# Moving small exponentials and a tiny transpose out of the start-up of a fused layer-norm, state-space and gated-linear kernel

## Chip, cores, metric

One core of one Trainium2 chip. The metric is the device time of one execution in microseconds (us), the median of several runs. Each ratio is taken against the kernel before in the same call.

Names: PE is the matmul engine, PEld its weight loads, DVE the vector engine, ACT the scalar (activation) engine, POOL GpSimd, SP the engine that only issues DMAs here.

## The reference, cut to what matters

```python
xn = layernorm(x)                       # x: 2048 x 576
# A: diagonal state-space layer
dt      = exp(log_dt)                   # 576 values
Lam_bar = exp(dt * (Lambda_re + 1j*Lambda_im))
B_bar   = ((Lam_bar - 1) / Lam)[:, None] * Bmat
h[t]    = Lam_bar * h[t-1] + B_bar @ xn[t]
A       = 2 * Re(Cmat @ h) + xn * Dskip
# B: gated linear unit
B       = (sigmoid(xn @ w_gate) * (xn @ w_up)) @ w_down      # 576 -> 4608 -> 576
out     = x + A + B
```

The modulus of `Lam_bar` is `exp(dt * Lambda_re)`: 576 numbers, held as a tile `r5` of 128 x 5 (`r` in the views). It is first read when the tables of sines are combined, long after the start.

## The kernel before

The gate/up matmuls of the first groups start as soon as the first two of 16 row tiles of x are normalised and transposed. PSUM holds four pairs of banks; each group of 128 hidden columns takes a pair, and ACT frees it by writing sigmoid(gate) and then u = xn @ w_up to SBUF. In the views, `pgu` is the PSUM of a group, `ptr` that of the transposes and `pd` that of the down product; `sT` and `uT` are ACT's two outputs, and `crows` and `cvals` the constants before and after their transposes. The program order of the start (cuts marked `...`):

```python
def consts_transpose(ps):          # log_dt, Lambda_re, Lambda_im: 27 rows of 64 -> columns
    for half in (slice(0, H), slice(H, P)):
        nc.tensor.transpose(ps[half, 0:3 * NH], crows[:], ident[0:3 * NH, 0:3 * NH])

def exp_first():
    nc.scalar.activation(dt[:], ldt, ACT.Exp)
    for a in range(NU):                                            # NU = 5
        nc.scalar.activation(r5[:, a:a + 1], lre[:, a:a + 1], ACT.Exp, scale=dt[:, a:a + 1])
...
busy(10, TB)                       # filler matmuls, so that PE reaches full speed
busy(6, P)
for tt in range(2):
    ln_stats(tt); ln_std(0, tt, tt + 1)
for tt in range(2):
    ln_recip(0, tt, tt + 1); ln_norm(tt, twice=False); start_transpose(tt)
busy(20, P)
start_copy(0, ...); ...            # ACT and DVE copy the transposes to xT
start_groups[0].mms(slice(0, 2 * P))
start_transpose(2); start_transpose(3)
start_groups[1].mms(slice(0, 2 * P))
...
start_groups[0].mms(slice(2 * P, TB))
consts_transpose(ptrs[1][:, NH, :])
consts_copy(ptrs[1][:, NH, :])     # DVE
start_groups[1].mms(slice(2 * P, TB))
for tt in range(TT_B, 2 * TT_B):
    ln_stats(tt)                   # DVE: statistics of the second block of x
for g in start_groups:
    g.evac()                       # ACT: sigmoid, copy of u; DVE: product
ln_std(1, 0, TT_B)                 # ACT: square root
exp_first()                        # ACT
...                                # then the other groups, f = 2, 3, ...
```

Far later, in the first down phase (`pd` matmuls, where ACT has little to do), `sines()` computes eleven sines on ACT.

## Time and profile before

| | before |
|---|---|
| median of the first three runs | 508.32 us (508.27 to 509.04) |
| span in the profile | 506.7 us |
| PE busy | 501.5 us |
| steady places where PE waits | one, at 22 us |

The prediction shows the lines that carry this. One more view will serve as a ruler: the timeline restricted to PE, from 9.3 us to the first down phase (its first row, the rest of group 0's first matmuls, is left out). Columns: start us, duration us, engine, line, operation, number merged, idle before and its cause.

```profile
9.79 1.20 PE L747 MATMUL ptr<-ident,xn 128*64 128x128 bf16 x36
10.92 2.14 PE L501 MATMUL pgu<-xT,wgu 64*128 64x256 bf16 x36
12.99 0.20 PE L196 MATMUL ptr<-ident,crows 27*64 27x27 bf16 x2
13.12 8.93 PE L501 MATMUL pgu<-xT,wgu 64*128 64x256 bf16 x90
22.88 35.14 PE L501 MATMUL pgu<-xT,wgu 64*128 64x512 bf16 x324 [0.83 <-ACT uT L508]
57.95 1.28 PE L575 MATMUL pd<-wd,hT 128*128 128x288 bf16 x9
```

From 10.92 on PE has work in hand without a break, except for the small transposes (L196) and the stop. I call the stretch from the first of these rows with L501 (10.92) to the first `pd` matmul (57.95) the stream. Its length is 57.95 - 10.92 = 47.03 us. It leaves out the start-up before it.

### The profile page before, as it was taken

To read this page: it belongs to the slowest core of one execution; us is meant where nothing else is said; L and a number is where in the kernel's file an instruction comes from. 1 tells how busy PE (TensorE), PEld (TensorE's weight loads), DVE (VectorE), ACT (ScalarE), POOL (GpSimd) and SP (SyncE) were. 2 spreads that over 40 slices of the span, in tenths; PEclk is the share of its full clock that TensorE was granted. 3 is DMA by queue.
4 is the path that set the end of the run, shared out by engine and by line. 5 is a ranking of instruction groups with operands and counts; after the bars stand their busy time and mean duration, and the time that the engine had idled before them with its cause. 6 is when DMAs were issued, how large, how long until landed. Compare 5 with 4: busy or idle time off the path is not lost.

```text
span 506.7 us, 10667 instructions
## 1 busy us (share of the span) xinstructions
PE 501.5 (99%) x4538; PEld 292.5 (58%) x4538; DVE 324.7 (64%) x705; ACT 204.4 (40%) x371; POOL 90.8 (18%) x134
## 2 busy tenths in 40 slices
PE   8999999999999999999999999999999999999997
PEld 6455675444477444467764444774444774446775
DVE  5799788887888587868588667786675222222111
ACT  4965723556500756530016655005655005553000
POOL 7116320123110043110001331100431001300000
PEclk9999999999999999999999999999999999999999
DMA  8897594065220096342340652100643200600101
GB/s 224 195 163 218 147 210 94 6 159 136 50 51 25 1 171 150 78 107 69 71 107 2 164 141 49 47 25 1 160 107 86 49 25 24 187 1 1 36 25 35
DMA packets 40949, 45.59 MB, mean 90 GB/s; under 512 B 28614, under 2 KB 32326, under 8 KB 40902
## 3 DMA queue, kind: packets, MB, share of 16 engines
q0 software_dynamic: 10608, 34.22, 27.5%
q1 hardware_dynamic: 29862, 10.37, 10.2%
q8 instruction: 35, 0.57, 0.5%
q10 hardware_dynamic: 432, 0.33, 0.2%
q14 instruction: 12, 0.10, 0.1%
HBM read 34.36 MB, written 2.36 MB: 72 GB/s over the span
## 4 chain that ended last, share of the span: by engine, by line
PE 97%; ACT 1%; DVE 1%; issue 0%
PE pgu L501 54%; PE pd L575 34%; PE pbu L530 7%; PE pd L583 1%; PE pgu L739 1%; DVE bnst L230 1%; PE ptr L747 0%; ACT xT L750 0%; ACT L507 0%; ACT L334 0%; ACT r L336 0%; DVE mv L231 0%; ACT uT L508 0%; ACT rstd L234 0%; DVE ob L584 0%
## 5 line engine op out<-in xcount | busy, mean ns | idle before, releaser
L501 PE MATMUL pgu<-xT,wgu 64*128 64x512 bf16 (+1 forms) x2628 | 284.1, 373 | 0.9 <-ACT uT L508 0.8
L501 PEld LDWEIGHTS <-wgu 64*128 64x128 bf16 x2628 | 130.2, 94 | 149.4 <-issue 1.6
L575 PE MATMUL pd<-wd,hT 128*128 128x288 bf16 x1128 | 141.3, 286 | 0.0
L507 ACT ACTIVATE sT<-pgu 128x512 bf16<-128x512 f32 x144 | 86.5, 600 | 120.0 <-PE pgu L501 119.1
L575 PEld LDWEIGHTS <-hT 128*128 128x128 bf16 x1128 | 109.9, 98 | 30.1 <-issue 0.8
L510 DVE TENSOR_TENSOR hT<-sT,uT 128x512 bf16<-128x512 bf16 x144 | 60.7, 422 | 95.0 <-ACT uT L508 94.7
L508 ACT CAST uT<-pgu 128x512 bf16<-128x512 f32 x144 | 84.2, 585 | 0.0
L154 POOL DMA_DIRECT2D wgu<-in_B_w_gate_dram x36 | 27.6, 766 | 236.4 <-PE pgu L501 224.7
L536 ACT COPY bure<-pbu 128x512 f32<-128x512 f32 x16 | 9.4, 585 | 88.8 <-PE pbu L530 75.0
L160 POOL DMA_DIRECT2D wd<-in_B_w_down_dram x36 | 26.3, 733 | 98.9 <-PE pd L575 98.8
L595 DVE TENSOR_TENSOR acc<-acc,pd 128x576 f32<-128x576 f32 x32 | 24.1, 752 | 27.6 <-PE pd L575 27.6
L592 DVE TENSOR_TENSOR ob<-acc,pd 128x576 bf16<-128x576 f32 x15 | 11.3, 755 | 40.9 <-PE pd L575 40.9
L530 PE MATMUL pbu<-xT,bt 64*128 64x512 bf16 x288 | 33.7, 376 | 0.0
L575 PEld LDWEIGHTS <-hst 128*128 128x128 bf16 x270 | 26.4, 98 | 6.7
L154 POOL DMA_DIRECT2D wgu<-in_B_w_up_dram x36 | 26.5, 736 | 1.3 <-DMA wgu<-in_B_w_up_dram 1.3
L445 DVE TENSOR_TENSOR_SCAN gre<-r,g0re,wrim 128x512 bf16<-128x512 f32 x20 | 25.6, 1279 | 0.1
L575 PE MATMUL pd<-ctre,hst 128*128 128x288 bf16 x120 | 24.5, 286 | 0.0
L575 PE MATMUL pd<-ctim,hst 128*128 128x288 bf16 x120 | 24.5, 286 | 0.0
L530 PEld LDWEIGHTS <-bt 64*128 64x128 bf16 x288 | 13.8, 94 | 17.1 <-issue 0.7
L452 DVE TENSOR_TENSOR_SCAN gim<-r,g0im,wrim 128x512 bf16<-128x512 f32 x16 | 20.4, 1276 | 0.0
L230 DVE BATCH_NORM_STATS2 bnst<-xt 128x6 f32<-128x288 bf16 x32 | 12.5, 432 | 2.3 <-DMA xt<-in_A_x_dram 2.3
L432 DVE TENSOR_TENSOR tq<-T,buim 128x512 bf16<-128x512 bf16 x20 | 13.7, 685 | 0.0
(117 smaller groups left out, 279.9 us busy)
## 6 DMA issues: line engine op xcount, KB each, us to landing
wgu<-in_B_w_gate_dram POOLq DMA_DIRECT2D x36, 288.0 KB, 4.1
wgu<-in_B_w_up_dram POOLq DMA_DIRECT2D x36, 288.0 KB, 4.7
wd<-in_B_w_down_dram POOLq DMA_DIRECT2D x36, 288.0 KB, 5.5
out_dram<-ob SPq DMA_DIRECT2D x15, 144.0 KB, 1.8
xt<-in_A_x_dram SPq DMA_DIRECT2D x10, 144.0 KB, 2.7
xt<-in_A_x_dram POOLq DMA_DIRECT2D x4, 144.0 KB, 6.7
bt<-ctre POOLq DMA_DIRECT2D x2, 288.0 KB, 6.0
bt<-ctim POOLq DMA_DIRECT2D x2, 288.0 KB, 7.5
```

The source lines that it names most:

```text
L154: eng.dma_start(w[rows, :, :], src[:, fs].rearrange("(c p) f -> p c f", p=H))
L160: nc.gpsimd.dma_start(wd[:], B_w_down[f0:f0 + FP * P, :].rearrange("(n p) d -> p n d", p=P))
L230: nc.vector.bn_stats(st[:, gi, :], xt[:, gi * DH:(gi + 1) * DH])
L445: nc.vector.tensor_tensor_scan(gre[:], r_bc, w[:, 0, :], g0re[:, col], ALU.mult, ALU.add)
L452: nc.vector.tensor_tensor_scan(gim[:], r_bc, w[:, 1, :], g0im[:, col], ALU.mult, ALU.add)
L501: nc.tensor.matmul(self.ps[:, gi, cols], w[rows, c, fs], xT[self.nb][rows, c, cols], start=c == 0, stop=c == NH - 1)
L507: nc.scalar.activation(sT[:], self.ps[:, 0, :], ACT.Sigmoid)
L508: nc.scalar.copy(uT[:], self.ps[:, 1, :])
L510: nc.vector.tensor_mul(h[:], sT[:], uT[:])
L530: nc.tensor.matmul(out, w, xT[self.nb][rows, c, ts_], start=c == 0, stop=c == NH - 1)
L575: nc.tensor.matmul(out, lhsT, rhs[:, a * DH:(a + 1) * DH], start=i == 0, stop=i == n - 1)
L595: nc.vector.tensor_add(halves(acc[:]), halves(acc[:]), pd[:, :, 0:DH])
```

## The change

Intent: take work that nobody needs yet off ACT's and DVE's way to the release of a PSUM pair. `exp(log_dt)` stays in front (DVE's angles need dt); `exp(dt*re)` becomes one DVE product in background work and one exponential ahead of the sines; the transposes of the constants run among the filler matmuls, so that DVE need not wait for them at 13 us.

```diff
     def exp_first():
         nc.scalar.activation(dt[:], ldt, ACT.Exp)
-        for a in range(NU):
-            nc.scalar.activation(r5[:, a:a + 1], lre[:, a:a + 1], ACT.Exp, scale=dt[:, a:a + 1])
 
     def angles_small():
+        nc.vector.tensor_mul(r5[:], dt[:], lre)
@@
     def sines():
+        nc.scalar.activation(r5[:], r5[:], ACT.Exp)
@@
-    busy(20, P)
+    consts_transpose(ptrs[1][:, NH, :])
+    busy(18, P)
@@
     start_groups[0].mms(slice(2 * P, TB))
-    consts_transpose(ptrs[1][:, NH, :])
     consts_copy(ptrs[1][:, NH, :])
```

## The prediction

> **What bounds the kernel now.** I read the busy shares first, then PE's waits, the chain that ended last, and the timeline around the one place where PE waits. From the page:
>
> ```profile
> PE 501.5 (99%) x4538; PEld 292.5 (58%) x4538; DVE 324.7 (64%) x705; ACT 204.4 (40%) x371; POOL 90.8 (18%) x134
> ```
>
> PE is busy for 501.5 of 506.7 us. A change that adds or removes no matmul of the main loop can win only where PE stands still. The list of waits names one such place in steady work:
>
> ```profile
> PE pgu L501 <- ACT uT L508: 0.8, 1, 0.8
> ```
>
> The same list restricted to PE after 25 us is empty: from there to the tail nothing that another engine does delays a matmul. So only the first 25 us count. The chain, in order of time, shows how they end (start, us, what):
>
> ```profile
> 10.99 2.07 PE pgu L501 x36
> 13.06 0.15 PE ptr L196 x2
> 13.21 0.02 issue
> 13.23 0.17 DVE cvals L201
> ...
> 17.32 0.22 DVE mv L231
> 17.54 0.02 issue
> 17.57 0.30 ACT rstd L234
> 17.87 0.02 issue
> 17.88 1.28 ACT L334
> ...
> 19.42 0.04 ACT r L336
> ...
> 20.46 1.28 ACT L507
> ...
> 22.25 0.59 ACT uT L508
> 22.84 0.04 issue
> 22.88 35.14 PE pgu L501 x324
> ```
>
> Read it backwards. PE resumes at 22.88 when ACT has copied out u of group f=2, because group f=6 needs that PSUM pair (four pairs: the two transpose tiles take the first two, groups 0 and 1 the others, f=2 to f=5 follow round, f=6 reuses the pair of f=2). ACT was late because it ran, in order, the square root of the second block's deviations, a table load, six exponentials and a table load. The square root was late because DVE had stood still for the constants' transpose, which PE ran only after the second half of group 0. Both parts of the change lie on this one chain.
>
> The timeline, cut to ACT and DVE rows (start, us, engine, line, idle before), gives the durations:
>
> ```profile
> 13.23 0.17 DVE L201 CAST cvals<-ptr 64x15 f32<-64x15 bf16 x1 [0.96 <-PE ptr L196]
> 17.57 0.30 ACT L234 ACTIVATE rstd<-mv,eps_t 128x4 f32<-128x4 f32 x1 [0.87 <-DVE mv L231]
> 19.18 0.21 ACT L334 ACTIVATE dt<-cvals 128x5 f32<-128x5 f32 x1
> 19.42 1.03 ACT L336 ACTIVATE r<-cvals,dt 128x1 f32<-128x1 f32 x5
> ```
>
> **What PE really loses.** The 0.83 us of idle in the record counts from the modelled end of the last matmul. By starts it is more: asked in narrow windows, matmuls of 512 columns start in pairs 0.216 us apart, the last pair before the stop at 21.66, so the next was due at 21.88. It started at 22.88: 1.00 us lost. In the same way the constants' transposes: the last pair of group 0 starts at 12.79, pairs of 256 columns come every 0.11, so the next was due at 12.90; it started at 13.12. The two tiny transposes cost PE 0.22 us there.
>
> **What the Trainium skill says.** "ScalarE: Activation LUTs", section What ACT_TABLE_LOAD costs: a load takes about 1283 ns and a drain of about 1380 ns comes with it. The trace agrees on the load (1.28 us each) but not on a drain: the load for L334 begins at 17.88, 0.01 after the square root ends, and dt starts at 19.18, 0.02 after the load. I use 1.28. The same section has back-to-back ACTIVATEs with one pointer operand at 280 ns, less 93 ns of overlap; the five here take 1.03/5 = 0.206 us each, near that difference. The section "Table sets: the hidden batching unit" says to batch by set, not to return to one: the change goes against this (Exp is used in two places now), so I charge one more load. "TensorE: Matmul & The Clock Gate", section Back-to-back issue gap, has 518 cycles for 512 columns, 0.216 us at 2.4 GHz; the pairs' starts agree.
>
> **The change part by part.**
>
> Part A, exponentials. Removed from the early ACT sequence: five at 1.03 us in all. Kept: dt (0.21) and both table loads, Exp and back to Sigmoid (1.28 each), so most of that block stays. On the way to the release of f=2's pair: -1.03 us. Added: one DVE product of 128x5 in the background work of the first group phase. Its neighbour, dt times lim, takes 0.16 us at 38.14, where PE waits for nothing: 0 on the path. Added in the first down phase: a load of Exp's set (1.28) and one exponential of 128x5 (0.21), so the ten sines of 128x512 come about 1.5 us later. There ACT has 16.89 us of idle after the sines (row of the next load, at 83.78). DVE first wants r5 and the small sines at 64.72; these were done at 60.75 and will be at about 62.3. Its first table product at 66.90 needs the first two large sines, then done by about 63.4; the last of ten moves from 66.88 to 68.4, and its reader comes after 79. All slack is over 2 us: 0 on the path.
>
> Part B, constants' transposes. They go from after group 0's second half to the filler ahead of group 0, in exchange for two filler matmuls of about 0.06 us. PE is 0.22 us shorter at 13 us. In the filler they may add 0.22 - 0.12 = 0.1, but the last filler starts at 8.40 and group 0 only at 8.70, after ACT's copy of xT ends at 8.66; 0.1 fits in. Their data were issued on the SP queue by 2.74; loads of that queue take 2.9 us to land, so about 5.6, before 7.3.
> DVE's 0.96 us of idle goes: the copies can start at 12.29 behind the last xT copy. The statistics follow without gaps, so their end moves from 17.54 to about 16.6. The x tiles issued by POOL from 4.53 to 6.2 land in at most 6.8 us, by 13.0 at the latest; the first is read at about 12.75 (landed about 11.2), the last at 15.6. No new wait. On ACT the second sigmoid, which waits for group 1, moves forward 0.1 (ACT is busy to 14.20), so the load of Sqrt's set ends at about 16.6 in place of 16.69, and the square root starts at about 16.62 in place of 17.57: -0.95 us.
>
> **Sum.** Release of the pair: 22.88 - 0.95 - 1.03 = 20.90. PE's need: 21.88 - 0.22 = 21.66. The release comes 0.76 us early, so the stop disappears: PE gains 1.00 + 0.22 = 1.22 us. The 1.98 us saved on ACT are not what is won; PE's own work is the new bound. The following groups need their pairs at intervals of 1.94 us while ACT releases one each 1.0 us, so no later stop forms. Everything after is PE back to back and shifts as a block. 508.32 - 1.22 = 507.10.
>
> Alone, A would give a release at 21.85 against a need at 21.88: gain 1.00. B alone 21.93 against 21.66: stop of 0.27, gain 1.22 - 0.27 = 0.95. So the parts overlap: 1.22, not 1.95.
>
> **Rivals.**
>
> 1. Another wait takes the early place, as the statistics waiting for x tiles in a DMA stage that is over 80% busy from 13 to 23 us. For it: DVE comes 0.94 us earlier. Against: the landing times above, and 0.76 us of margin. If DVE gained nothing, release would be at 21.85 against 21.66: 0.2 of stop, time about 507.3.
>
> 2. The delayed sines stop DVE in the down phase; accumulations come late and PE lacks PSUM. For it: the work of 1.5 us is real, and DVE is busy for 19.4 of 23.7 us there. Against: over 2 us of slack at the first reader and four pairs in rotation. If all of it reached PE: -1.22 + 1.5, 508.6.
>
> 3. The transposes in the filler hold up the first group, by their data or by the switch of tile shape, and push the whole chain. Against: 0.25 us of slack there. If 0.2 leaked, 507.3. A lower clock through two fewer fillers would cost more, but the slices grant full clock throughout and 18 fillers stay.
>
> 4. PE is not really bound after 25 us in a way the chain hides. Against: the empty list.
>
> **Range and chances.** The three runs of before spread from 508.27 to 509.04, two of them 0.05 apart, so a median should repeat within some 0.2; the possible leaks of 0.2 each lie on the slow side, a run in the upper mode adds up to 0.7 to one run only. I take 507.1 us, 506.7 to 507.9. Two per cent are 10.2 us, eight times what is at stake: same 0.98, 0.01 on either side.
>
> **What would show it.** Right: no wait of PE for uT around 22 us; DVE's copies of the constants at about 12.3 without idle; the square root at about 16.6; one ACTIVATE of r 128x5 in the first down phase behind a table load of its own, with ACT idle of about 15.4 us left after the sines; start of the first down phase's matmuls at about 56.7 in place of 57.95; twelve table loads in place of eleven in all. Wrong: a new PE wait below 25 us or between 57 and 84 us; a first matmul of group 0 later than 8.75; a gain of 1.0 or less though the stop is gone, which would mean that the 0.22 of the transposes was paid elsewhere; a gain near 2, which would mean that the release and not PE set the time.

## The result, and the profile after

The changed kernel took 507.58 us (median of 6 runs, 507.21 to 507.84) against 508.65 us (6 runs, 508.27 to 509.04) for the kernel before. The ratio is 0.9979, interval 0.9966 to 0.9992: 1.07 us. Ratios here and below are the mean time of one kernel's runs over that of the other's of the same rounds, so not quite the ratio of the quoted medians.

The page of the changed kernel, first row, to be held against PE's 501.5 us:

```profile
PE 500.9 (99%) x4536; PEld 289.6 (57%) x4536; DVE 324.6 (64%) x706; ACT 204.8 (40%) x368; POOL 90.8 (18%) x134
```

PE's timeline of the changed kernel from 9.3 us, the same view as above:

```profile
10.12 1.20 PE L747 MATMUL ptr<-ident,xn 128*64 128x128 bf16 x36
11.25 45.86 PE L501 MATMUL pgu<-xT,wgu 64*128 64x256 bf16 x450
57.04 2.13 PE L575 MATMUL pd<-wd,hT 128*128 128x288 bf16 x16
```

The transposes at 13 us and the stop are gone; 450 matmuls run as one piece. The stream is 57.04 - 11.25 = 45.79 us, 1.24 us shorter. But it starts 0.33 us later. The reason stands in the timeline from 6 to 24 us (PE, ACT and DVE rows, cut):

```profile
5.96 1.23 PE L747 MATMUL ptr<-ident,xn 128*64 128x128 bf16 x36
...
7.79 0.20 PE L196 MATMUL ptr<-ident,crows 27*64 27x27 bf16 x2 [0.60 <-DMA crows<-in_A_Lambda_im_dram]
...
8.03 0.69 ACT L750 COPY xT<-ptr 128x640 bf16<-128x640 bf16 x1 [0.22 <-PE ptr L196]
...
9.04 1.16 PE L501 MATMUL pgu<-xT,wgu 64*128 64x256 bf16 x18
...
12.52 0.16 DVE L201 CAST cvals<-ptr 64x15 f32<-64x15 bf16 x1
...
16.85 0.30 ACT L234 ACTIVATE rstd<-mv,eps_t 128x4 f32<-128x4 f32 x1
17.17 1.28 ACT L334 ACT_TABLE_LOAD   x1
...
18.46 0.21 ACT L334 ACTIVATE dt<-cvals 128x5 f32<-128x5 f32 x1
18.67 1.28 ACT L507 ACT_TABLE_LOAD   x1
...
20.46 0.58 ACT L508 CAST uT<-pgu 128x512 bf16<-128x512 f32 x1
```

In this execution the constants' loads landed late, PE waited 0.60 us for them in the filler, and group 0 started at 9.04. Behind that, all goes as foreseen: DVE copies the constants without idle, the square root starts without waiting for the statistics, and u of group f=2 is out at 21.04.

What the change added in the first down phase, ACT's timeline from 57 to 84 us, without its first two rows:

```profile
58.24 1.28 ACT L359 ACT_TABLE_LOAD   x1
59.54 0.21 ACT L359 ACTIVATE r<-r 128x5 f32<-128x5 f32 x1
59.75 1.28 ACT L360 ACT_TABLE_LOAD   x1
61.05 0.31 ACT L360 ACTIVATE sc<-sc,zero_t 128x20 f32<-128x20 f32 x1
61.26 6.22 ACT L364 ACTIVATE sctab<-sctab,zero_t 128x512 f32<-128x512 f32 x10
82.87 1.28 ACT L507 ACT_TABLE_LOAD   x1 [15.38 <-PE pgu L501]
```

One load and one exponential more, 15.38 us of idle left. The list of PE's waits names nothing after 8 us.

So two questions went to the chip. Is the sum of the prediction right (two overlapping gains, then PE's own work as the bound)? And does the new place of the transposes cost time regularly, or was the wait of 0.60 us a matter of this one execution?

### The profile page after: what moved, and what is told of

It is laid out like the page before. It is cut to its first block, busy times and chain, and to the rows that moved or that the text cites. A ratio compares the mean times of both kernels' runs of the same rounds, so it can differ in the third digit from the quotient of the medians.

```text
span 505.7 us, 10662 instructions
## 1 busy us (share of the span) xinstructions
PE 500.9 (99%) x4536; PEld 289.6 (57%) x4536; DVE 324.6 (64%) x706; ACT 204.8 (40%) x368; POOL 90.8 (18%) x134
## 4 chain that ended last, share of the span: by engine, by line
PE 98%; DMA 1%; SPq 0%; issue 0%; DVE 0%
PE pgu L501 55%; PE pd L575 34%; PE pbu L530 7%; DMA crows<-in_A_Lambda_im_dram 1%; PE pd L583 1%; PE ptr L747 0%; PE pgu L739 0%; SPq L139 0%; SPq L192 0%; DVE ob L584 0%; PE ptr L196 0%
## 5 line engine op out<-in xcount | busy, mean ns | idle before, releaser
L501 PEld LDWEIGHTS <-wgu 64*128 64x128 bf16 x2628 | 127.7, 94 | 150.9 <-issue 0.5
L431 DVE TENSOR_TENSOR wrim<-T,bure 128x512 bf16<-128x512 bf16 x20 | 13.7, 684 | 0.0
```

What stands on the lines that cost most here:

```text
L431: nc.vector.tensor_mul(w, t1, a[:])
L501: nc.tensor.matmul(self.ps[:, gi, cols], w[rows, c, fs], xT[self.nb][rows, c, cols], start=c == 0, stop=c == NH - 1)
```

## Experiments

Before the single runs, the ruler over all profiles. The release of the pair that group f=6 takes is the moment when ACT has emptied it; the need is the moment when PE would start on it if nothing held it. The need is the start of the stream plus 10.73 us (in run e8 below the stream starts at 11.07 and the pair after the last unhindered one was due at 21.80).

| run | stream starts | stream length | against 47.03 | median time | ratio to before |
|---|---|---|---|---|---|
| before | 10.92 | 47.03 | | 508.65 | |
| e12, before again | 11.09 | 47.03 | 0 | 508.70 (one run) | |
| the change | 11.25 | 45.79 | -1.24 | 507.58 | 0.9979 |
| e5, the change again | 11.32 | 45.79 | -1.24 | 507.40 | 0.9975 |
| e1, exponentials alone | 11.31 | 46.02 | -1.01 | 507.88 | 0.9984 |
| e2, transposes alone | 11.52 | 45.95 | -1.08 | 507.97 | 0.9986 |
| e3, constants' loads earlier | 13.97 | 46.30 | -0.73 | 508.61 | 1.0015 |
| e4, transposes in PE's gap | 10.86 | 45.79 | -1.24 | 507.33 | 0.9977 |
| e6, 6 fillers | 10.76 | 45.79 | -1.24 | 507.28 | 0.9974 |
| e7, 4 exponentials back | 10.74 | 46.54 | -0.49 | 507.41 | 0.9977 |
| e8, 9 exponentials | 11.07 | 46.69 | -0.34 | 508.21 | 0.9992 |
| e9, short first fillers | 12.51 | 45.79 | -1.24 | 508.16 | 0.9986 |
| e10, e4 and e9 together | 12.39 | 45.79 | -1.24 | 508.17 | 0.9992 |
| e11, later sines | 10.85 | 45.79 | -1.24 | 507.35 | 0.9977 |

Where nothing holds it, the stream repeats to 0.01 us. Its start moves by up to 0.8 us between profiles with the same opening (10.74 in e7, 11.52 in e2): that is where the scatter of the times sits. All experiments gave correct results.

### e1, the exponentials alone

```diff
+    busy(20, P)
-    consts_transpose(ptrs[1][:, NH, :])
-    busy(18, P)
@@
+    consts_transpose(ptrs[1][:, NH, :])
     consts_copy(ptrs[1][:, NH, :])
```

(against the changed kernel)

> Only the exponentials are moved; the constants' transposes stay at 13 us. Theory L (the filler position makes PE wait about 0.6 us for the constants' loads, which eats what part B gives): the stop before f=6 goes (release about 21.85 against a need of 21.88), gain 1.0 us over before, so as fast as the whole change within 0.15 us; group 0 starts 2.5 us after the first transpose as before, no PE wait for crows. Rival S (the sum of the prediction holds, 1.22, and 0.3 of it was lost to scatter of the start): gain 1.0 as well, but then the whole change measured in the same call should be 0.2 us faster than this.

PE's timeline of e1:

```profile
11.31 2.14 PE L501 MATMUL pgu<-xT,wgu 64*128 64x256 bf16 x36
13.38 0.20 PE L196 MATMUL ptr<-ident,crows 27*64 27x27 bf16 x2
13.51 43.89 PE L501 MATMUL pgu<-xT,wgu 64*128 64x256 bf16 x414
57.33 1.89 PE L575 MATMUL pd<-wd,hT 128*128 128x288 bf16 x14
```

The stop is gone and the transposes at 13 us remain. The stream is 46.02 us: 1.01 won of the 1.00 predicted for this part. It is 0.23 us longer than the changed kernel's, which is the cost of the two transposes in that place (0.22 predicted). Here the start was late without any wait for the constants: the first transposes began at 6.27 and took 1.37 us. By the clock e1 won 0.8 us (ratio 0.9984, interval 0.9972 to 0.9996), less than the ruler says; by the sum above, that is a start 0.2 us later on average (an estimate from the mean times).

### e2, the transposes alone

```diff
     def exp_first():
         nc.scalar.activation(dt[:], ldt, ACT.Exp)
+        for a in range(NU):
+            nc.scalar.activation(r5[:, a:a + 1], lre[:, a:a + 1], ACT.Exp, scale=dt[:, a:a + 1])
 ...   # and the DVE product and the late exponential taken out again
```

> Only the constants' transposes are moved; six exponentials stay in front. Theory L: PE waits about 0.6 us for crows in the filler as in the changed kernel, the square root starts without waiting for the statistics, release about 1.03 us later than in the changed kernel, a stop of about 0.1 us at f=6; gain over before 0.6 to 0.9 us. Rival S: gain 0.95 us with a stop of 0.27 us and no or a shorter wait for crows. If the parts simply added, this would gain 0.1 to 0.2 us only.

The list of PE's waits showed none at 22 us, but the starts of pairs did; PE's timeline of e2, asked in two narrow windows that overlap the same matmuls (the first row merges the pair at 22.03 with one of the next pair):

```profile
22.03 0.74 PE L501 MATMUL pgu<-xT,wgu 64*128 64x512 bf16 x3
22.40 0.39 PE L501 MATMUL pgu<-xT,wgu 64*128 64x512 bf16 x2
```

Pairs come every 0.216 us, so the one after 22.03 was due at 22.25; it came at 22.40. A stop of 0.15 us is there, hidden in the record by the modelled end of the matmul before it. The stream is 45.95 us: 1.08 won, against 0.95 predicted with a stop of 0.27. Alone the parts win 1.01 and 1.08, together 1.24: they overlap as predicted, and adding them (2.09) would be wrong.

### e3, the constants' loads issued earlier

```diff
-    for tt in range(TT_B):
-        load_x(tt, nc.sync if tt % 2 == 0 else nc.scalar)
+    for tt in range(2):
+        load_x(tt, nc.sync if tt % 2 == 0 else nc.scalar)
+    crows = ...  # its three loads on the SP queue, moved up from below
+    for tt in range(2, TT_B):
+        load_x(tt, nc.sync if tt % 2 == 0 else nc.scalar)
```

> The whole change, with the three small loads of the constants issued between the two x tiles of the SP queue in place of after them, so about 0.5 us earlier and ahead of more of the weights. Theory L: the wait of PE for crows shrinks from 0.60 us to 0.2 or nothing, group 0 starts 2.5 to 2.7 us after the first transpose (3.08 in the changed kernel, 2.50 before), gain over before 1.2 to 1.5 us. Rival S: the start stays as it is, 1.07 us over before. Risk: x tile 2 lands about 0.9 us later, but it is read only at 6.4 us.

508.61 us (6 runs, 508.38 to 510.99), ratio 1.0015: a miss. There are two kinds of runs: four of 508.38 to 508.65 and two of 510.82 and 510.99. The profile is of the 510.82. Its timeline (SP, PE and DVE rows, cut):

```profile
2.29 0.36 SPq L139 DMA_DIRECT2D xt<-in_A_x_dram  x1
...
7.23 0.20 PE L198 MATMUL ptr<-ident,crows 27*64 27x27 bf16 x2
...
8.56 0.27 PE L503 MATMUL pgu<-xT,wgu 64*128 64x256 bf16 x1
8.93 0.82 DVE L232 BATCH_NORM_STATS2 bnst<-xt 128x6 f32<-128x288 bf16 x2 [2.38 <-DMA xt<-in_A_x_dram]
```

The constants were there in time and group 0 began 2.50 us after the first transposes (6.06 to 8.56), as expected. But the x tile that stood behind them, issued at 2.29 in place of 1.2, landed 6.6 us later (DVE reads it at 8.93). In the profiles read, the x tiles issued on SP before 1.6 us land in 2.8 to 3.1 us; this one, issued a microsecond later, took more than twice that, with POOL's weight loads issued from 1.45 on (whether these are the cause was not tested). So the risk named in the expectation came true, and larger. It is not all: group 0 stopped after one matmul, 0.57 us for weights and later 1.14 us for xT, and behind these pauses the granted clock of this profile reads 0.50 from 12 to 15 us and the next 36 transposes took 2.13 us. The stream started at 13.97 and, partly at half clock, took 46.30 us. The other slow run has the same mean clock (0.997) in its record. The four faster runs, still about 1.1 us slower than e4, have no profile.

### e4, the transposes in a gap of PE

```diff
-    consts_transpose(ptrs[1][:, NH, :])
-    busy(18, P)
+    busy(20, P)
@@
     start_groups[0].mms(slice(0, 2 * P))
+    consts_transpose(ptrs[1][:, NH, :])
     start_transpose(2)
```

(against the changed kernel)

> The exponentials moved, the constants' transposes placed right ahead of the third x tile's transposes, where PE waits 0.2 us for DVE anyway and the loads have landed; 20 fillers again. Theory L: no wait for crows, group 0 starts 2.5 us after the first transpose, the transposes cost PE 0 to 0.15 us there, no stop at f=6: gain over before 1.05 to 1.25 us, 0.1 or more faster than the whole change. Rival S: no difference from the whole change.

507.33 us (5 runs), ratio 0.9977, interval 0.9965 to 0.9989. The transposes ran at 9.60 with no wait, 0.13 us ahead of the third tile's; the stream was 45.79 us. The change again had 0.9975. No difference that these runs can show, so the half of the theory that said the filler place costs time regularly got no support here.

### e5, the change again

No edit.

> The changed kernel unaltered, for comparison on this chip. Theory L: its profile again shows the constants' transposes starting at about 7.7 us, whatever moment the first transposes start at (5.96 to 6.3), because the landing of the constants' loads sets it; group 0 starts at 9.0 to 9.1; gain over before 0.9 to 1.1. Rival S (the wait was a matter of one run): transposes at 7.2 to 7.5 and group 0 at 8.6 to 8.7.

507.40 us (5 runs, 506.96 to 507.70), ratio 0.9975, interval 0.9963 to 0.9988: 1.27 us by the ratio, 1.17 us between the medians (508.57 before). The timeline of PE in the first 9 us:

```profile
6.27 1.43 PE L747 MATMUL ptr<-ident,xn 128*64 128x128 bf16 x36
7.63 0.20 PE L196 MATMUL ptr<-ident,crows 27*64 27x27 bf16 x2
```

The constants' transposes start at 7.63 as the theory wanted, but there is no wait for a DMA before them: PE itself came late, with first transposes at 6.27 that took 1.43 us. e2, e6, e7, e8 and e11 have the same instructions as the change up to here, and their transposes of the constants ran at 7.74, 7.21, 7.19, 7.47 and 7.30 with no wait. So the wait of 0.60 us appeared in one of seven profiles with this opening. In e5 and e2 PE came so late that the loads may have landed at 7.66 as before; e6, e7, e8 and e11 decide, where they had landed earlier. My theory that the landing of these loads sets the start each time has fallen. What made them late in that one execution stays open.

### e6, fewer fillers

```diff
-    busy(18, P)
+    busy(6, P)
```

> The changed kernel with 6 fillers in place of 18 behind the constants' transposes. If PE's queue of fillers, set back by the wait, is what holds group 0, then group 0 starts with the end of ACT's copy of xT, about 8.75 in place of 9.04, and the time falls by 0.3 us against the changed kernel of the same call. If ACT's copy holds it (it waits for the constants' transposes too, 0.22 us in the profile), nothing changes. Risk: fewer fillers leave the clock lower, then it is slower.

507.28 us (5 runs) against 507.40: the same. In its profile no wait for constants occurred, PE ran out of fillers and waited 0.7 us for ACT's copy, and group 0 began at 8.55, 2.50 us after the first transposes. As the wait that it was built to bypass did not occur, it doesn't decide what would hold group 0 after such a wait; it shows that 12 fillers more or fewer here don't matter.

### e7 and e8, exponentials put back by the dose

```diff
     def exp_first():
         nc.scalar.activation(dt[:], ldt, ACT.Exp)
+        for a in range(4):      # e7; range(9) in e8
+            nc.scalar.activation(r5[:, a % NU:a % NU + 1], lre[:, a % NU:a % NU + 1], ACT.Exp, scale=dt[:, a % NU:a % NU + 1])
```

(against the changed kernel; r5 is overwritten later, so results stay right)

> The changed kernel with four of the five single exponentials put back in front (their results are overwritten later): 0.82 us more on ACT. Theory M (release of f=2's pair is now ahead of PE's need by about 0.9 us): same time as the changed kernel within 0.15 us, no gap in the matmul pairs around 22 us. Rival N (ACT's sequence still sets the time): 0.8 us slower.

> The changed kernel with nine single exponentials in front: 1.85 us more on ACT. Theory M: a gap in the matmul pairs of 1.85 - 0.9 = 0.9 us around 22 us and 0.8 to 1.0 us slower than the changed kernel, so as slow as before. Rival N: 1.85 us slower.

Four exponentials: 507.41 us (5 runs) against 507.40. Its stream is 0.75 us longer in the profile, but not at 22 us: PE's timeline of e7 shows another wait.

```profile
10.74 7.22 PE L503 MATMUL pgu<-xT,wgu 64*128 64x256 bf16 x91
18.33 39.02 PE L503 MATMUL pgu<-xT,wgu 64*128 64x512 bf16 x359 [0.37 <-DMA wgu<-in_B_w_up_dram]
```

This execution started its stream early, at 10.74, and met the weights of group f=4 not yet landed. Even without that delay the release fits: u of f=2 left ACT at about 21.4, and the need was 10.74 + 10.73 = 21.47. So for four the equal time is the evidence, and the profile only agrees with it.

Nine exponentials: 508.21 us (5 runs), 0.81 us slower than the change. PE's timeline of e8 around 22 us, the first row from a narrow window:

```profile
21.58 0.38 PE L503 MATMUL pgu<-xT,wgu 64*128 64x512 bf16 x2
22.68 0.39 PE L503 MATMUL pgu<-xT,wgu 64*128 64x512 bf16 x2 [0.72 <-ACT uT L510]
```

Due at 21.80, started at 22.68: 0.88 us lost, with 0.9 expected. The stream is 0.90 us longer. This is the full dose curve: 0 exponentials cost nothing, 4 nothing by the clock, 5 (run e2) 0.16 us, 9 cost 0.90 us. Past the threshold four more exponentials cost 0.74 us, and ACT's rows in the two traces differ by just that (nine take 1.77 us in e8, five 1.03 in e2), so there ACT's work sets the time. The threshold is the margin of release against need: in the changed kernel 11.25 + 10.73 = 21.98 needed, 21.08 released (u out at 21.04, and 0.04 to PE as before), 0.90 us.

### e9 and e10, fewer fillers at the very start

```diff
-    busy(10, TB)
-    busy(6, P)
+    busy(8, TB)
+    busy(4, P)
```

(e9 against the change, e10 against e4)

> The changed kernel with 8 long and 4 short fillers at the very start in place of 10 and 6. In four of nine profiles so far these 16 matmuls, at the low starting clock, ran to 6.3 us and set back the first transposes, whose data are there at 6.0. Theory W (what varies between runs is the start: clock of PE in the first 6 us and landing of loads; from the start of the unbroken PE stream at about 11 us to the first down phase it is 45.79 us whenever nothing waits): first transposes at 6.0, stream from 10.7 to 10.9, 45.79 us again, 0.1 to 0.3 us faster than the changed kernel's 507.4 to 507.6. Rival C: fewer fillers, the clock rises later, transposes take 1.5 instead of 1.2 us, no gain or a loss.

> The same shorter start with the constants' transposes ahead of the third tile's transposes (run e4). Theory W: 45.79 us for the stream, start at about 10.8; as fast as e9 or 0.1 slower, since the transposes take 0.13 us of PE on the way there. Theory L, much weakened by e5 to e7 (no wait for the constants' loads in their profiles): 0.2 us or more faster than e9.

Both went wrong: 508.16 (4 runs: 508.88, 507.25, 508.71, 507.60) and 508.17 us (508.74, 509.14, 507.19, 507.60). Two kinds of runs. PE's timeline of e9, a run of 508.88:

```profile
6.18 2.13 PE L747 MATMUL ptr<-ident,xn 128*64 128x128 bf16 x36 [0.91 <-DVE xn L255]
...
8.41 1.96 PE L739 MATMUL pgu<-warm 128*128 128x128 bf16 x18
10.30 1.16 PE L501 MATMUL pgu<-xT,wgu 64*128 64x256 bf16 x18
```

36 transposes took 2.13 us in place of 1.20 to 1.23, 18 fillers 1.96 in place of 1.18: PE ran at about half speed until 10 us. The profile of e10, a run of 508.74, shows the same (2.13 us, 20 fillers in 1.90); the other slow runs and the fast ones have no profile. The idle gap of 0.91 us ahead of the transposes is not enough to explain it: e4 idled 0.78 us there and its transposes took 1.23. But its 16 fillers had taken 3.99 us, so PE had reached full speed before the gap, while the 12 of e9 took 4.02 us, so it had not. The Trainium skill, "TensorE: Matmul & The Clock Gate", section What's actually happening, describes it: PE starts at half clock and rises after some 3.4 us of sustained activity, and a window that runs freely shifts the moment from run to run. The trace agrees with half speed and with the scatter (the same 16 fillers, from 1.25 us on, took 3.99 us in e4 and 5.09 us in e5). Of the two expectations that of rival C, the clock, came true (it had put the transposes at 1.5 us). That the window is the reason is the page's account; no run here shows it. The last fillers of the first batch look superfluous where they run beyond 6.0 us, but without them four of eight runs were about 1.5 us slower. From 12.51 us on the stream of e9 was 45.79 us again.

### e11, the sines set back further

```diff
     def sines():
         nc.scalar.activation(r5[:], r5[:], ACT.Exp)
+        scr = consts.tile([P, NU], FP32, name="scr")
+        for _ in range(2):
+            nc.scalar.activation(scr[:], thc[:], ACT.Sin, bias=zero_t[:], scale=SIN_SCALE)
+            nc.scalar.activation(scr[:], dt[:], ACT.Exp)
```

> The changed kernel with two more switches Sin, Exp on scratch tiles between the late exponential and the sines: four loads of 1.28 us and four small ACTIVATEs, some 6 us more on ACT in the first down phase (four times what the change added). Theory (ACT idles 15.4 us there, four PSUM pairs absorb DVE's delay of some 3.5 us): first down phase of PE still 23.63 us, no slower than the changed kernel within 0.2. Rival 2 of the prediction: PE waits for PSUM, up to several us slower.

507.35 us (4 runs, 507.23 to 507.43), ratio 0.9977. Two rows of its timelines in the first down phase (ACT, DVE) and one of the chain:

```profile
66.90 0.31 ACT L364 ACTIVATE sc<-sc,zero_t 128x20 f32<-128x20 f32 x1
67.24 0.17 DVE L373 TENSOR_TENSOR nr<-r,sc 128x5 f32<-128x5 f32 x1 [3.75 <-ACT sc L364]
```

```profile
56.71 23.63 PE pd L579 x192
```

The small sines moved from 61.05 (changed kernel) to 66.90, and DVE now did stand still for them, 3.75 us; yet PE's down phase is 23.63 us, as in every other profile. DVE's delay did not reach PE; that the four PSUM pairs took it up is my reading. With five times the delay that the change added here (the small sines start 10.26 us after the first `pd` matmul, against 4.01 in the changed kernel and 2.49 before) the down phase is no longer.

### e12, the kernel before again

No edit.

> The kernel before, one more profile, for the start. Theory W: stream from its start (10.7 to 11.4, as with the others) to the first down phase 47.03 us again, with the stop before f=6. If the change itself delays the start, this starts at 10.9 or earlier.

508.70 us. PE's timeline:

```profile
11.09 2.14 PE L501 MATMUL pgu<-xT,wgu 64*128 64x256 bf16 x36
...
23.05 35.14 PE L501 MATMUL pgu<-xT,wgu 64*128 64x512 bf16 x324 [0.83 <-ACT uT L508]
58.12 2.13 PE L575 MATMUL pd<-wd,hT 128*128 128x288 bf16 x16
```

58.12 - 11.09 = 47.03 us again. Its stream starts at 11.09, with no change made. The streams of the six profiles that run as the change does up to their start begin at 11.25, 11.52 (e2), 11.32 (e5), 10.74 (e7), 11.07 (e8), 10.85 (e11), mean 11.13; the three that run as the kernel before does at 10.92, 11.31 (e1) and 11.09, mean 11.11. The change doesn't move the start by an amount that these few profiles can show.

## Why the prediction was right

The time, 507.58 us against 507.1 predicted, lies in the range, and "same" is right. Of the 0.48 us between them 0.33 is the starting point (508.32 was the median of three runs, all six have 508.65) and 0.15 is the gain, 1.07 in place of 1.22. Point by point:

- **PE waits in one place only.** Right: with that stop removed, the stream runs as one piece of 45.79 us in every profile in which neither ACT's dose nor a weight load held it.
- **What PE loses by starts, not by the recorded idle.** Right: 1.00 + 0.22 = 1.22 us predicted, 1.24 us shorter stream. The recorded idle of 0.83 us alone would have given 1.05.
- **Part A alone 1.00.** 1.01 (e1). **Part B alone 0.95.** 1.08 (e2). Here two terms were mis-sized: the stop that B leaves was put at 0.27 us and was 0.15 to 0.16. I had DVE's copies of the constants begin behind the last copy of xT, 1.37 us after the stream's start; in the profile of the change they overlap with it and begin 12.52 - 11.25 = 1.27 us after it. And I had ACT's second sigmoid move forward by 0.1 us only, because ACT was busy with u before it; in the profile it overlaps with u and moved by 0.23 us (14.32 - 10.92 before, 14.42 - 11.25 after). So the statistics and the table load, which both hold the square root, ended about 0.1 us earlier than I had put them.
- **The parts overlap.** Right, and the margin of 0.76 us by which the release should precede the need was 0.90.
- **The late exponential is free.** Right, and with a wide margin (e11).
- **The transposes fit in the filler.** Half right. "Loads of that queue take 2.9 us to land, so about 5.6" was a wrong step: it applied the landing time of loads issued before 1.6 us to loads issued at 1.7 to 2.7 us. In the profile of the change they came at 7.7 us and PE waited 0.60 us. My own sign of a failure, "a first matmul of group 0 later than 8.75", came true there at 9.04. But it was a poor sign: the kernel before has 8.88 in its second profile (e12), and e1, with the transposes in their old place, 8.94. No lasting cost is seen: in six other profiles of the same opening there was no such wait.
- **The down phase at 56.7.** It came at 57.04 in that profile: the 1.24 us less 0.33 us of later start.
- **Rivals.** The first (statistics waiting for x tiles) didn't happen. The second fell with e11. The third, by its data, happened once. Its argument from the clock ("the slices grant full clock throughout") was no proof: in e9 the granted clock reads 1.00 where PE ran at half speed. The fourth fell with the constant stream and the constant rest of 450.57 us.

What is left between 1.07 us (first call), 1.27 us (second call) and 1.24 us (stream) is scatter of the start. Worked back from the mean times (an estimate: mean less stream less 450.57), the changed kernel started at 11.21 in the first call and at 11.03 in the second, the kernel before at 11.05 and 11.04. The runs show two sources of that scatter: when PE's clock rises, and when loads land. Which of them made the first call's 0.16 us stays open, since only one of its six runs has a profile. No version beat the change clearly: e4, e6 and e11 are within its scatter.

## What to carry to other kernels

When an engine is nearly always busy, measure a stop by when the next instruction was due, not by the recorded idle, and compare savings upstream with the margin between release and need: what is saved beyond the margin wins nothing, and two savings on one chain don't add. Work moved into a phase where its engine idles can be free; a deliberate overdose in one run shows with what reserve. To judge a change of a microsecond in a kernel with a noisy start, find a stretch whose length repeats exactly and compare that; a wait seen in a single profile of the start is not yet a cost.

## What the Trainium skill lacked or had wrong

- "ScalarE: Activation LUTs", What ACT_TABLE_LOAD costs: the drain of about 1380 ns per switch doesn't appear. A load takes 1.28 us, begins where the ACTIVATE before it ends (18.46 + 0.21, then 18.67), and the next ACTIVATE starts 0.01 to 0.02 us after its end in the three switches shown above (17.17 + 1.28, then 18.46). Budgeting 2.66 us would have been double.
- "TensorE: Matmul & The Clock Gate" has the slow start and its scatter (and the trace agrees); what would help is the size at the edge: with four filler matmuls fewer, four of eight runs were about 1.5 us slower, and the two of them that have a profile show PE at half speed until 10 us. The granted clock reads 1.00 throughout these two profiles, so only durations show it (2.13 us for 36 transposes in place of 1.23); in e3, after PE had run at full speed and paused, it reads 0.50 for the same duration.
- "DMA: Bandwidth & Descriptors", Latency and other measured facts, gives a fixed cost of about 2 us. A small load issued at 2.4 us behind some weight loads took 5.25 us to land (7.66) in one profile and at most 4.8 us in e6 and e7 (used at 7.2), an x tile issued at 2.29 us took 6.6 us, the same kind of tile issued before 1.6 us took 2.8 to 3.1 us. I found no figure in it for how landing grows with what is already queued.
